# Filler matmuls in three widths, a truer count of busy PSUM banks and new priorities in a planned two-layer spectral and feed-forward kernel

## The chip, the cores and the metric

The kernel runs on one core of one Trainium2 chip. A core has five engines with queues of their own, each served in order: TensorE (PE in the profile; its weight loads are PEld), VectorE (DVE), ScalarE (ACT), GpSimd (POOL) and SyncE (SP), which issues most DMAs. Products of TensorE land in PSUM, which has 8 banks of 512 float32 columns by 128 partitions; ACT and DVE copy them from there to SBUF. The metric is the device time of one launch in microseconds, the median of several runs.

## The reference

The input x has 2048 rows (tokens) of 448 numbers. Two kinds of layer alternate, A, B, A, B, each with a residual:

```python
def _A_ref(x, w_r, w_i):              # spectral filter
    X = rfft2(x.astype(float32), axes=(-2, -1))
    X = X * (w_r + 1j * w_i)
    return irfft2(X, s=(S, D), axes=(-2, -1)).astype(bfloat16)

def _B_ref(x, w1, b1, w2, b2):        # feed-forward, 448 -> 1792 -> 448
    h = einsum("bsd,df->bsf", x, w1) + b1
    r = where(h > 0, h, 0)
    return einsum("bsf,fd->bsd", r * r, w2) + b2

x = x + _A_ref(_layernorm(x), A_w_r, A_w_i)
x = x + _B_ref(_layernorm(x), B_w1, B_b1, B_w2, B_b2)
x = x + _A_ref(_layernorm(x), A_w_r, A_w_i)
x = x + _B_ref(_layernorm(x), B_w1, B_b1, B_w2, B_b2)
```

The Fourier transform runs over all tokens, so a spectral layer needs the last token of the layer before it.

## The kernel before

The transforms are products with constant matrices, all in bf16 with float32 sums in PSUM. The 2048 tokens are 16 tiles of 128. A spectral layer goes through these steps, each a few matmuls into a PSUM tile and a copy out of it on ACT or DVE (`EV` says which engines may take it):

- A1 (first layer) or A2 (second): a first radix step over the tokens, with the layer norm's factor folded into the matrix `Fs`; result `XA`.
- TD: the transform over the 448 columns, per frequency pair p; result `U`.
- B: the second radix step; result `EF`.
- W: the product with the complex weights, on DVE alone; result `Z`. M mirrors half of the weights for it, in the first layer.
- Bi: the inverse of B; result `VT`.
- TI and AI: the inverse of the column transform (copied out to `tmp` by ACT) and of the first radix step, for one or two token tiles at a time, added to the residual x_sb on DVE at L994. ln: the layer norm's numbers, the transpose of these tokens into `yT` (matmuls with `J_sb` for the first two token tiles, DMA transposes for the others).

The feed-forward goes through h (hidden blocks of 128: four groups c of four token tiles; the first group in two halves, `h0.0.0` and `h0.0.2`, with matmuls of 256 columns; the others in pairs of half-height matmuls of 512 columns; ReLU on ACT at L631, square on DVE at L666) and o (per token tile 14 matmuls of 448 columns; the sum with the residual on DVE at L1135). In the first feed-forward, A2 of a token tile follows on its o. In the second, its rows are stored.

Nothing of the order on an engine is written out. The program is first recorded as operations (`_Op`) with their true dependencies, grouped in units (`_Unit`; a unit of PE is the chain of matmuls into one PSUM tile or a few), each with a cost in ns. `schedule` then plays the kernel through in planned time. At each step it looks, per engine, at the units whose predecessors are placed, works out when each could start (operands ready, engine free, for PE a bank free), keeps those within `look` of the earliest, and takes the one with the highest priority. A unit's priority is the longest planned path behind it, plus a bias by kind of step and layer (`PR`), plus an adjustment by its tag (`ADJ`; the tag `TI0.4` is step TI, layer 0, token tile 4; `h0.0.0` layer 0, group 0, half 0). Priority counts only among units that may start at nearly the same time. The bank of a PSUM tile is picked in the same loop (`pick_banks`), from the planned time `bank_free` at which each bank comes free. On the chip, the first matmul into a tile waits for the true readers of the tile that had the bank before.

The same loop puts in dummy matmuls: when PE's next unit starts long after PE is free, it inserts matmuls of a block of ones (`warm_mm`, L1238) into a free bank. Nothing reads them; they keep TensorE active. `used` holds the planned times in which PE was at work, dummies included. `cold_until` is 8000 ns: before that, the plan takes a dummy at twice its time.

Of the kernel before, what the change touches and what calls it, by code (L numbers as in the profile page):

```python
# [34 lines left out]
def make_constants():  # L35
# [64 lines left out]
    for g, M in enumerate((cl * np.cos(th), cl * np.sin(th))):  # L100
# [8 lines left out]


PR = {'A1': 65800.0, 'A1step': 7500.0, 'TD': [48800.0, -113100.0], 'B': [36300.0, -23900.0], 'W': [76300.0, 35800.0], 'Bi': [21700.0, 28400.0], 'step': [16400.0, 1100.0], 'M': 33500.0, 'aux': -104400.0, 'ramp': [210200.0, 192900.0], 'rstep': [2800.0, 6700.0], 'late': [85200.0, 100700.0], 'lstep': [5400.0, 6200.0], 'TI': [53500.0, 42800.0], 'AI': [44600.0, 400.0], 'h': [57700.0, -6500.0], 'A2': -27100.0, 'xb': 113100.0}
ADJ = {"": 6701, "A1.0": 29257, "A1.1": 17447, "A1.2": 16379, "A1.3": 23248, "A1.4": 19707, "A1.5": 21681,
       "A1.6": 23426, "A1.7": 1783, "A2.0": 3983, "A2.1": 24182, "A2.10": -59216, "A2.11": -3532, "A2.12": -36244,
       "A2.13": -45335, "A2.14": 47820, "A2.15": 139734, "A2.2": 1038, "A2.3": -3066, "A2.4": -12568, "A2.5": -8452,
       "A2.6": -4047, "A2.7": 1978, "A2.8": 10431, "A2.9": 63588, "AI0.0": 68353, "AI0.1": 897, "AI0.10": 516,
       "AI0.12": -5956, "AI0.14": -67415, "AI0.2": -38654, "AI0.4": -19829, "AI0.6": -15078, "AI0.8": -3605,
       "AI1.0": -20686, "AI1.1": 5286, "AI1.10": 1100, "AI1.12": -1141, "AI1.14": 13691, "AI1.2": 8647,
       "AI1.4": 59291, "AI1.6": 54430, "AI1.8": 6345, "B0.0": 19136, "B0.1": 115640, "B0.2": 22993, "B0.3": 75809,
       "B0.4": 5158, "B0.5": -4397, "B0.6": -8848, "B0.7": -51758, "B1.0": -113802, "B1.1": -60488, "B1.2": -51246,
       "B1.3": -110840, "B1.4": -102695, "B1.5": -50678, "B1.6": 21521, "B1.7": -91417, "Bi0.0": 96550,  # L120
       "Bi0.1": 144608, "Bi0.2": -84722, "Bi0.3": 90659, "Bi0.4": 115575, "Bi0.5": 64595, "Bi0.6": 43560,
       "Bi0.7": 5502, "Bi1.0": 27868, "Bi1.1": 58049, "Bi1.2": 174789, "Bi1.3": 85322, "Bi1.4": 51663,
       "Bi1.5": 84773, "Bi1.6": 122291, "Bi1.7": 95285, "M.0": -32582, "M.1": -77962, "M.2": -68639, "M.3": 11620,
       "M.4": -46400, "M.5": -52498, "M.6": -28578, "TD0.0": 62885, "TD0.1": 53127, "TD0.2": 30685, "TD0.3": 20599,
       "TD0.4": 45748, "TD0.5": 6280, "TD0.6": -18691, "TD0.7": -26835, "TD1.0": -26881, "TD1.1": -47123,
       "TD1.2": -62851, "TD1.3": -61189, "TD1.4": -81728, "TD1.5": -152870, "TD1.6": -80437, "TD1.7": -77952,
       "TI0.0": 37017, "TI0.1": -736, "TI0.10": -2254, "TI0.12": 51203, "TI0.14": 50504, "TI0.2": -15325,
       "TI0.4": 50369, "TI0.6": 10302, "TI0.8": -66186, "TI1.0": 4491, "TI1.1": 3839, "TI1.10": -18554,
       "TI1.12": -107791, "TI1.14": -62712, "TI1.2": -15113, "TI1.4": 24227, "TI1.6": -31726, "TI1.8": -63713,
       "W0.0": -3627, "W0.2": 11084, "W0.4": -35444, "W0.6": -72978, "W0.7": -86496, "W1.0": 87646, "W1.2": 77648,  # L130
       "W1.4": 114799, "W1.6": 49655, "W1.7": 28094, "aux": -45173, "h0.0.0": 19527, "h0.0.2": 78856,
       "h0.1.0": 106321, "h0.2.0": -90133, "h0.3.0": 65659, "h1.0.0": 15793, "h1.0.2": 2885, "h1.1.0": 56706,
       "h1.2.0": 30843, "h1.3.0": 25208, "ln0.0": 12199, "ln0.1": -1793, "ln0.10": 5272, "ln0.12": 6757,
       "ln0.14": -2830, "ln0.2": 61906, "ln0.4": 6787, "ln0.6": -5943, "ln0.8": -612, "ln1.0": 1193, "ln1.1": 5862,
       "ln1.10": 30854, "ln1.12": 26593, "ln1.14": -57295, "ln1.2": 10235, "ln1.4": -19457, "ln1.6": 28337,
       "ln1.8": 65496, "o0.0": -10899, "o0.1": -31999, "o0.10": -18100, "o0.11": -15446, "o0.12": -23168,
       "o0.13": -7449, "o0.14": -17614, "o0.15": -23139, "o0.2": -32228, "o0.3": -23571, "o0.4": -25779,
       "o0.5": -21180, "o0.6": -19238, "o0.7": -16528, "o0.8": -28787, "o0.9": -21480, "o1.0": 41922, "o1.1": -13364,
       "o1.10": 16273, "o1.11": 113849, "o1.12": 38097, "o1.13": 61656, "o1.14": 72389, "o1.15": 26660,
       "o1.2": 24314, "o1.3": -19452, "o1.4": 54106, "o1.5": -30131, "o1.6": 31837, "o1.7": -19040, "o1.8": 49988,  # L140
       "o1.9": 20532, "xbln0.0": -1222, "xbln0.1": -297, "xbln0.10": -57869, "xbln0.12": -15841, "xbln0.14": 4467,
       "xbln0.2": -3853, "xbln0.4": -57430, "xbln0.6": -22322, "xbln0.8": -3189, "xbln1.0": -17529,
       "xbln1.1": -10627, "xbln1.10": -2861, "xbln1.12": 67706, "xbln1.14": 22722, "xbln1.2": -8750,
       "xbln1.4": -9401, "xbln1.6": 58720, "xbln1.8": -23621}
STAY = 3000.0
LOOK = {'act': 0.0, 'dve': 50.0, 'pe': 0.0}
EV = {'A1': ['act'], 'A2': ['act'], 'TD': ['act', 'dve'], 'B': ['act', 'dve'], 'Bi': ['act', 'dve'], 'Bi0': ['act', 'dve'], 'TI': ['act'], 'M': ['act', 'dve'], 'T': ['act', 'dve'], 'XR': ['pool'], 'FS': ['pool'], 'FS2': ['dve'], 'XN': ['act', 'dve']}
SPLIT = (1, 2, 4)
NFLIP = 2
# [2 lines left out]


class _Op:
    __slots__ = ("eng", "fn", "deps", "has_dep", "ticket", "is_dma", "dsem", "cost", "lat", "unit", "gdeps", "alt", "tile")

    def __init__(self, eng, fn, is_dma, cost, lat):
        self.eng = eng
        self.fn = fn
        self.deps = []  # L160
        self.gdeps = []
        self.has_dep = False
        self.ticket = None
        self.is_dma = is_dma
        self.dsem = None
        self.cost = cost
        self.lat = lat
        self.unit = None
        self.alt = None
        self.tile = None  # L170

    def semkey(self):
        if self.is_dma:
# [61 lines left out]
class _Sched:  # L235
# [6 lines left out]
    DMA_RATE = 400.0  # L242
    TURN = 100.0
    BEGIN = 800.0

    def __init__(self):
        self.ops = {e: [] for e in self.ENGINES}
# [12 lines left out]
    def add(self, eng, fn, reads=(), writes=(), is_dma=False, cost=100.0, lat=130.0, unit=None):  # L260
# [32 lines left out]
        for a in reads:  # L293
            if isinstance(a, _PsAP):
                a.tile.readers.append(op)
        op.unit = u
        u.ops.append(op)
        return op
# [9 lines left out]
    def schedule(self):  # L308
# [88 lines left out]
        while total:  # L397
# [25 lines left out]
            if e == "pe":  # L423

                while self.warm_fn is not None:
                    gap = start - free["pe"]
                    recent = sum(min(b, free["pe"]) - max(a, free["pe"] - 3400.0) for a, b in used[-60:]
                                 if b > free["pe"] - 3400.0)
                    cold = free["pe"] < self.cold_until
                    unit = 430.0 if cold else 216.0  # L430
                    if gap < unit + (150.0 if cold or recent < self.warm_share * 3400.0 else 700.0):
                        break
                    bk = pick_banks(1, free["pe"])
                    if bk is None:
                        break
                    if bk[0] > free["pe"]:
                        free["pe"] = bk[0]
                        continue
                    d = _Op("pe", self.warm_fn(bk[1]), False, unit, 195.0)
                    old = bank_user[bk[1]]  # L440
                    if old is not None:
                        d.deps.extend(old.readers)
                    if not self.ops["pe"]:
                        d.deps.extend(self.warm_deps)
                    self.ops["pe"].append(d)
                    used.append((free["pe"], free["pe"] + unit))
                    free["pe"] += unit
                start = max(start, free["pe"] + (self.TURN if u.rows != rows else 0.0))
                rows = u.rows
# [20 lines left out]
            for op in u.ops:  # L470
# [3 lines left out]
                if op.is_dma:  # L474
                    dma_free = max(dma_free, t + 1800.0) + op.lat
                    done[op] = dma_free
                for a in (op.gdeps if e != "pe" else ()):
                    if a.tile is not None:
                        for i in range(a.tile.bank, a.tile.bank + a.tile.n):
                            bank_free[i] = max(bank_free[i], t + op.lat)  # L480
            if e == "pe":
                used.append((start, t))
            free[e] = t
            for v in order[u]:
                left[v] -= 1
                if left[v] == 0:
                    enter(v)
        self.length = max(done.values())
        self.done = done
        for e in self.ENGINES:  # L490
            for op in self.ops[e]:
# [32 lines left out]
def bass_interleave_layers__spectral_gfnet__dense_activation_squared_relu__prompt_kernel(nc, A_x, A_w_r, A_w_i, B_x, B_w1, B_b1, B_w2, B_b2, out):  # L524
# [6 lines left out]
    with ExitStack() as es:  # L531
# [702 lines left out]
        ffn(True)  # L1234


        def warm_mm(b):
            return lambda e: e.matmul(ps[:, b, :], ones[:], ones[:, None, :].to_broadcast([P, 4, P]), start=True,  # L1238
                                      stop=True)

        sch.warm_fn = warm_mm
# [75 lines left out]
```

## Time and the profile before

| what | value |
|---|---|
| median of 3 runs | 283.35 us (282.05 to 284.42) |
| profiled execution, time | 282.04 us |
| profiled execution, span | 279.5 us |
| mean granted TensorE clock | 0.994 |
| busy PE, DVE, ACT, POOL | 262.2, 213.5, 182.1, 13.2 us |
| dummy matmuls | 18 |

The span goes from the first to the last instruction of the program. The busy time of PE counts matmuls with modelled ends; they are pipelined, so a matmul of 256 columns has a duration of 0.28 us in a row while one follows another every 0.11 to 0.12 us. A chain line names the engine and line that the end waited for, followed back from the last instruction. In a row of a table by stage, the figures are the stretch, its length, the busy time and count of instructions for each engine, the granted TensorE clock as a share of full speed, the busy share of the DMA engines and GB/s. L612 is the helper that records every matmul, L637 and L638 are the copies out of PSUM on ACT and on DVE or POOL, and L666 is the helper for two-operand arithmetic.

### The profile page before, as it was taken

The numbers are of one execution on the slowest core, as the hardware profiler recorded it, in microseconds if no ns is written. First come the engines' busy times: TensorE is split into PE (matmuls) and PEld (weight loads), VectorE is DVE, ScalarE is ACT, GpSimd is POOL, SyncE is SP. The second block draws the span as 40 slices with busy tenths as digits, with TensorE's granted clock in tenths as the row PEclk, the third lists the DMA queues.
The fourth block names the chain that finished last, engine by engine and source line by source line (L and its number), as shares of the span: only waits on it lengthen the run. The fifth ranks groups of instructions, "written<-read, shape, count | busy, mean of one in ns | idle before, by whom it ended". The sixth has DMA issues, their size and how long they took to land.

```text
span 279.5 us, 5600 instructions
## 1 busy us (share of the span) xinstructions
PE 262.2 (94%) x2021; PEld 161.9 (58%) x2024; DVE 213.5 (76%) x740; ACT 182.1 (65%) x386; POOL 13.2 (5%) x28
## 2 busy tenths in 40 slices
PE   7699998799999999999997879879999999999996
PEld 2487745578655445586556545658855444554444
DVE  5958997989999977946998799399999775221542
ACT  2598986989568994376215998699836987000830
POOL 5840000000000000000000000000000000000000
PEclk9999999979999999999999999999999999999999
DMA  7999700020133030000000000002044230111001
GB/s 262 339 381 308 181 9 0 2 39 18 22 79 71 8 70 0 2 1 2 0 0 0 2 0 4 0 4 39 18 93 105 38 75 2 49 35 49 0 20 49
DMA packets 28543, 16.61 MB, mean 59 GB/s; under 512 B 21826, under 2 KB 27170, under 8 KB 28388
## 3 DMA queue, kind: packets, MB, share of 16 engines
q1 hardware_dynamic: 28084, 15.50, 20.5%
q10 hardware_dynamic: 432, 0.75, 0.7%
q8 instruction: 16, 0.26, 0.4%
q14 instruction: 11, 0.09, 0.1%
HBM read 10.75 MB, written 1.84 MB: 45 GB/s over the span
## 4 chain that ended last, share of the span: by engine, by line
PE 77%; DVE 13%; ACT 4%; DMA 2%; issue 2%; POOL 0%; ACTq 0%; DVEq 0%; POOLq 0%
PE ps L612 77%; DVE tmp L666 6%; DMA FA_sb<-c_FA 2%; DVE arena L666 2%; ACT arena L637 1%; DVE x_sb L994 1%; ACT tmp L637 1%; DVE x_sb L1135 1%; DVE W_sb L749 1%; ACT VT L1018 1%; DVE st L768 0%; DVE yT L638 0%; ACT VT L637 0%; DVE arena L638 0%; POOL Fs L649 0%
## 5 line engine op out<-in xcount | busy, mean ns | idle before, releaser
L612 PE MATMUL ps<-yT,W_sb 64*128 64x512 bf16 (+1 forms) x770 | 91.2, 349 | 0.7 <-DVE yT L638 0.4
L612 PE MATMUL ps<-W_sb,arena 128*128 128x448 bf16 (+1 forms) x476 | 86.8, 341 | 0.0
L612 PEld LDWEIGHTS ps<-yT,W_sb 64*128 64x128 bf16 (+1 forms) x770 | 54.9, 96 | 33.3 <-ACT arena L631 1.9
L631 ACT ACTIVATE arena<-ps,b1col 128x512 bf16<-128x512 f32 x84 | 52.2, 686 | 28.6 <-PE ps L612 28.5
L612 PEld LDWEIGHTS ps<-W_sb,arena 128*128 128x128 bf16 x476 | 46.0, 98 | 37.4 <-DVE arena L666 1.0
L666 DVE TENSOR_TENSOR arena<-arena 128x512 bf16<-128x512 bf16 (+1 forms) x140 | 49.7, 369 | 21.4 <-ACT arena L631 20.9
L1135 DVE SCALAR_TENSOR_TENSOR x_sb<-ps,arena 128x448 bf16<-128x448 f32 (+1 forms) x26 | 15.3, 588 | 23.4 <-PE ps L612 23.0
L637 ACT ACTIVATE arena<-ps 128x896 bf16<-128x896 f32 (+1 forms) x37 | 24.9, 746 | 2.4 <-PE ps L612 2.3
L631 ACT ACTIVATE mv<-mv,epst 128x2 f32<-128x2 f32 (+1 forms) x38 | 11.3, 299 | 22.5 <-DVE mv L769 20.9
L637 ACT ACTIVATE XA<-ps 128x512 bf16<-128x512 f32 x32 | 17.6, 594 | 9.8 <-PE ps L612 9.7
L1018 ACT ACTIVATE VT<-x_sb 128x448 bf16<-128x448 bf16 x32 | 18.3, 573 | 6.3 <-DVE x_sb L994 6.0
L637 ACT ACTIVATE VT<-ps 128x512 bf16<-128x512 f32 (+1 forms) x32 | 17.2, 590 | 4.9 <-PE ps L612 4.7
L631 ACT ACTIVATE arena<-ps 128x256 bf16<-128x256 f32 x56 | 18.5, 399 | 2.2 <-PE ps L612 1.5
L666 DVE TENSOR_TENSOR tmp<-tmp,Wt 128x896 bf16<-128x896 bf16 (+1 forms) x32 | 15.9, 560 | 0.0
L612 PE MATMUL ps<-yT,VT 64*128 64x512 bf16 x42 | 15.8, 376 | 0.0
L612 PE MATMUL ps<-arena,G_sb 128*128 128x448 bf16 (+1 forms) x72 | 14.0, 332 | 1.6 <-ACT arena L637 1.0
L637 ACT ACTIVATE tmp<-ps 128x896 bf16<-128x896 f32 (+1 forms) x18 | 14.1, 829 | 1.6 <-PE ps L612 1.6
L612 PE MATMUL ps<-HS_sb,arena 128*128 128x512 bf16 x61 | 14.8, 380 | 0.2
L612 PE MATMUL ps<-TI_sb,VT 112*128 112x112 bf16 (+1 forms) x128 | 9.8, 224 | 3.6 <-DVE VT L638 0.7
L994 DVE SCALAR_TENSOR_TENSOR x_sb<-ps,x_sb 128x448 bf16<-128x448 f32 x16 | 9.4, 619 | 3.3 <-PE ps L612 3.3
L658 ACT ACTIVATE arena<-x_sb,mv,rstd 128x448 bf16<-128x448 bf16 x10 | 7.6, 759 | 5.7 <-DMA yT<-arena 4.1
L768 DVE BATCH_NORM_STATS2 st<-xin 128x6 f32<-128x448 bf16 x16 | 9.4, 606 | 2.3 <-DMA xin<-in_A_x_dram 2.3
(84 smaller groups left out, 309.7 us busy)
## 6 DMA issues: line engine op xcount, KB each, us to landing
out_dram<-x_sb SPq DMA_DIRECT2D x15, 112.0 KB, 1.7
W_sb<-in_B_w_dram SPq DMA_DIRECT2D x1, 1568.0 KB, 15.3
W_sb<-in_B_w_dram SPq DMA_DIRECT2D x1, 1344.0 KB, 11.4
HS_sb<-c_HS SPq DMA_DIRECT2D x1, 1024.0 KB, 6.0
xin<-in_A_x_dram SPq DMA_DIRECT2D x2, 448.0 KB, 5.7
G_sb<-c_G SPq DMA_DIRECT2D x1, 672.0 KB
xin<-in_A_x_dram ACTq DMA_DIRECT2D x1, 448.0 KB, 5.8
yT<-in_A_w_r_dram SPq DMA_DIRECT2D x1, 392.0 KB
```

The lines of the kernel that those rows point to most:

```text
L612: return sch.add("pe", lambda e: e.matmul(_res(o), lhsT, rhs, start=start, stop=stop, skip_group_check=skip), [lhsT, rhs], [o], cost=cost, ...
L631: sch.add("act", lambda e: e.activation(o, _res(i), func, **kw), rd, [o], cost=c)
L637: op = sch.add(engs[0], lambda e: e.activation(o, _res(i), ACT.Copy) if h[0].eng == "act" else e.tensor_copy(o, _res(i)), [i], [o], cost=c ...
L658: op = sch.add(engs[0], lambda e: e.activation(o, i, ACT.Identity, bias=b, scale=s) if h[0].eng == "act" else e.tensor_scalar(o, i, s, b, ...
L666: sch.add(eng, lambda e: e.tensor_tensor(o, _res(a), b, op), [a, b], [o], cost=_free(o) / rate + 69.0)
L749: small(lambda e, c=c, lo=lo: e.scalar_tensor_tensor(out=lo, in0=_res(c), scalar=-1.0 / D, in1=lo, op0=ALU.mult, op1=ALU.subtract), [c, lo ...
L768: small(lambda e, si=si, xi=xi: e.bn_stats(si, xi), [xi], [si], _free(xi) / 0.96 + 69.0)
L994: small(lambda e, xx=xx, xi=xi, r=r, i=i: e.scalar_tensor_tensor(out=xx, in0=_res(r), scalar=1.0, in1=xi, op0=ALU.mult, op1=ALU.add, accum ...
L1018: sch.add("act", lambda e, i=i, o=o, x=x: e.activation(o, x, ACT.Square, accum_out=sd[:, i, 1:2]), [x], [o, sd[:, i, 1:2]], cost=560.0)
L1135: small(lambda e: e.scalar_tensor_tensor(out=o, in0=_res(i), scalar=r[0] if r else 1.0, in1=xb[:, t, d0:d1], op0=ALU.mult, op1=ALU.add), [ ...
```

## The change

Four things change; the operations and their dependencies stay.

- Dummy matmuls come in 512, 256 or 128 columns. The plan looks at the use of PE in the 3413 ns (`WINDOW`) before the next unit's start, the gap itself counted as empty. Where that is under 70% (`warm_share`, unchanged), or in the cold start, it fills every gap of at least 120 ns with the widest dummy that leaves 60 ns. Where it is 70% or more, it puts in none.
- A bank is busy until the operations that read its tile end (`takes`). Before, each operation of another engine held up the banks of all matmuls among its dependencies, those with which it shares only an SBUF buffer included, and for a bank that meanwhile belonged to another tile too.
- All adjustments of `ADJ` are new, and some ten times larger.
- `LOOK` for PE goes from 0 to 50 ns.

```diff
-ADJ = {"": 6701, "A1.0": 29257, ...
+ADJ = {"": -580138, "A1.0": 899030, ...
-       "AI1.0": -20686, ... "TI0.2": -15325, "TI0.4": 50369, ... "TI1.4": 24227, ...
+       "AI1.0": -14810, ... "TI0.2": -21187, "TI0.4": -62986, ... "TI1.4": -1225233, ...
-       "h0.0.0": 19527, "h0.0.2": 78856, ... "ln1.0": 1193, ... "ln1.2": 10235, ...
+       "h0.0.0": 783048, "h0.0.2": 600819, ... "ln1.0": 976430, ... "ln1.2": 2049490, ...
 STAY = 3000.0
-LOOK = {'act': 0.0, 'dve': 50.0, 'pe': 0.0}
+LOOK = {'act': 0.0, 'dve': 50.0, 'pe': 50.0}
...
+    WINDOW = 3413.0
...
         for a in reads:
             if isinstance(a, _PsAP):
                 a.tile.readers.append(op)
+                op.takes.append(a.tile)
...
                 while self.warm_fn is not None:
                     gap = start - free["pe"]
-                    recent = sum(min(b, free["pe"]) - max(a, free["pe"] - 3400.0) for a, b in used[-60:]
-                                 if b > free["pe"] - 3400.0)
                     cold = free["pe"] < self.cold_until
-                    unit = 430.0 if cold else 216.0
-                    if gap < unit + (150.0 if cold or recent < self.warm_share * 3400.0 else 700.0):
+                    recent = sum(min(b, start) - max(a, start - self.WINDOW) for a, b in used[-90:]
+                                 if b > start - self.WINDOW)
+                    if gap < 120.0 or not (cold or recent < self.warm_share * self.WINDOW):
                         break
-                    bk = pick_banks(1, free["pe"])
+                    n = next((n for n in (512, 256, 128) if (n / 2.4 + 2.5) * (2.0 if cold else 1.0) + 60.0 <= gap), 0)
+                    bk = pick_banks(1, free["pe"]) if n else None
                     if bk is None:
                         break
                     if bk[0] > free["pe"]:
                         free["pe"] = bk[0]
                         continue
-                    d = _Op("pe", self.warm_fn(bk[1]), False, unit, 195.0)
+                    unit = (n / 2.4 + 2.5) * (2.0 if cold else 1.0)
+                    d = _Op("pe", self.warm_fn(bk[1], n), False, unit, 195.0)
...
-                for a in (op.gdeps if e != "pe" else ()):
-                    if a.tile is not None:
-                        for i in range(a.tile.bank, a.tile.bank + a.tile.n):
-                            bank_free[i] = max(bank_free[i], t + op.lat)
+                for w in op.takes:
+                    for i in range(w.bank, w.bank + w.n):
+                        bank_free[i] = max(bank_free[i], t + op.lat)
...
-        def warm_mm(b):
-            return lambda e: e.matmul(ps[:, b, :], ones[:], ones[:, None, :].to_broadcast([P, 4, P]), start=True,
+        def warm_mm(b, n):
+            return lambda e: e.matmul(ps[:, b, 0:n], ones[:], ones[:, None, :].to_broadcast([P, n // P, P]), start=True,
                                       stop=True)
```

The longest remaining path enters every priority, and `PR` and the constants in the program (22,000 per group for h, 5,500 per token tile for o) are as before.

## What I predict, and why

> **What bounds the kernel now.** I read the page first (busy shares, the row of the granted clock, the chain that ended last), then cut the span into stages and asked for the busy time of each.
>
> ```profile
> PE 262.2 (94%) x2021; PEld 161.9 (58%) x2024; DVE 213.5 (76%) x740; ACT 182.1 (65%) x386; POOL 13.2 (5%) x28
> PEclk9999999979999999999999999999999999999999
> PE 77%; DVE 13%; ACT 4%; DMA 2%; issue 2%; POOL 0%; ACTq 0%; DVEq 0%; POOLq 0%
> ```
>
> TensorE is busy for 94% of the span and holds 77% of the chain. One slice of the clock row is below 9. The chain leaves TensorE for DVE and ACT in short pieces only. The table by stage shows where (columns: stretch, length, busy time and instructions of PE, PEld, DVE, ACT and POOL, granted clock, DMA share, GB/s).
>
> ```profile
> 0.00:8.80 8.80, 5.37 (x16) 1.94 (x16) 5.34 (x19) 2.08 (x4) 4.77 (x12) 1.00 0.80 296
> 8.80:47.00 38.20, 36.56 (x273) 25.95 (x275) 33.44 (x91) 33.39 (x64) 8.46 (x17) 1.00 0.69 203
> 47.00:56.60 9.60, 7.07 (x87) 5.86 (x88) 7.33 (x37) 8.65 (x20) 0.00 (x0) 1.00 0.01 2
> 56.60:60.10 3.50, 3.50 (x20) 2.52 (x18) 3.08 (x11) 2.75 (x7) 0.00 (x0) 0.51 0.39 75
> 60.10:147.80 87.70, 87.34 (x666) 53.20 (x664) 75.54 (x300) 55.24 (x125) 0.00 (x0) 1.00 0.11 22
> 147.80:154.20 6.40, 4.37 (x53) 3.91 (x51) 5.09 (x24) 3.80 (x8) 0.00 (x0) 1.00 0.00 0
> 154.20:179.20 25.00, 21.91 (x165) 12.51 (x167) 21.52 (x49) 21.14 (x35) 0.00 (x0) 1.00 0.01 2
> 179.20:187.80 8.60, 6.74 (x84) 5.58 (x84) 6.48 (x30) 7.76 (x18) 0.00 (x0) 1.00 0.00 1
> 187.80:277.10 89.30, 89.30 (x668) 50.39 (x668) 55.28 (x182) 47.26 (x108) 0.00 (x0) 1.00 0.18 44
> ```
>
> The two feed-forward stages (60.1 to 147.8 and 187.8 to 277.1) are solid: 87.34 of 87.70 and 89.30 of 89.30. No order of work takes time out of them while their matmuls stay the same. Idle PE lies in five places: 38.20 - 36.56 = 1.64 in the first spectral layer, 2.53 in its ramp into the feed-forward (47.0 to 56.6), 2.03 at the layer boundary, 3.09 in the second spectral layer, 1.86 in its ramp: 11.15 us in all, beside 8.8 us before the first real matmul and 2.4 us behind the last. In the stretch 56.6 to 60.1 PE is never idle, but the clock is 0.51.
>
> **The clock dip.** The windows around it, and the matmuls in it:
>
> ```profile
> 49.80:53.20 3.40, 2.75 (x38) 1.00 0.02 5
> 53.20:56.60 3.40, 1.55 (x20) 1.00 0.00 0
> 152.20:155.60 3.40, 1.80 (x30) 1.00 0.02 5
> L612 PE MATMUL ps<-yT,W_sb 128*128 128x256 bf16 x16 | 3.5, 408 | 0.0
> L612 PE MATMUL ps<-yT,W_sb 128*128 128x256 bf16 x224 | 26.6, 282 | 0.4 <-DVE yT L638 0.4
> ```
>
> PE was busy for 1.55 of the 3.40 us just before the dip. [...] The price two ways: 3.50 x (1 - 0.51) = 1.7 us of lost clock; and 16 matmuls of 256 columns cover 3.5 us where the average over all 224 is 26.6 / 224 = 0.119 us, so 1.9 us: 1.6 lost. What follows is solid to 147.8, so the whole 1.7 us stands on the path.
>
> **The change, part by part.**
>
> *Dummies by recent use.* Before, one width (512 columns), only in a planned gap of at least 366 ns after low use, or 916 ns after high use. After: any planned gap of at least 120 ns, in the widest of 512, 256 and 128 that leaves 60 ns, as long as the planned use of the last 3413 ns, the gap counted as empty, is under 70%; above that none. The kernel before issues 18:
>
> ```profile
> L1238 PE MATMUL ps<-ones 128*128 128x512 bf16 x18 | 6.0, 496 | 1.9 <-POOL ones L679 1.9
> 1.88 5.37 PE L1238 MATMUL ps<-ones 128*128 128x512 bf16 x16 [1.88 <-POOL ones L679]
> 153.07 0.40 PE L612 MATMUL ps<-Fs,tmp 128*128 128x128 bf16 x4 [1.05 <-DVE tmp L675]
> L612 PE MATMUL ps<-Fs,tmp 128*128 128x128 bf16 x64 | 5.4, 219 | 1.3 <-DVE tmp L675 1.0 <-DVE x_sb L1135 0.2
> ```
>
> 16 stand at the start, two later, and none in the ramp before the dip. At the start nothing changes much: they fill time before the first data. A 128-column matmul costs (0.40 - 0.22) / 3 = 0.06 us of PE, its weight load beside it. The troughs hold 11.15 us of idle time, so at most some 180 dummies of the narrowest width. Cover: they lie in time in which PE waits for DVE and ACT, so I take 0 for them. Without that cover (the operand comes earlier on the chip than planned) the next real matmul waits for the rest of one dummy, 0 to 0.06 us of a narrow one. Each dummy also waits for the readers of the tile that its bank held, and everything on PE is queued behind it; as the plan takes that bank as free, I take 0 here too. Upper bound for both: 96 fills (11.15 / 0.116, a narrow dummy and its 60 ns) of 0.06 us, 5.8 us. What they bring: the ramp before the dip goes from 1.55 of 3.40 busy towards 70%, above the 1.80 that brought no dip; the boundary is filled by the same rule. I take the whole 1.7 us.
>
> *The bank count.* Before, each ACT, DVE or POOL instruction marked as busy the banks of every matmul it depends on, also of those whose SBUF operand it only overwrites, long after that bank had gone to another tile. After, it marks the banks it reads. No instruction or wait on the chip goes with this; the real waits were by true readers already. It only makes the plan truer, in the stretches where banks decide. The waits of PE in the ramp and in the second spectral layer:
>
> ```profile
> PE ps L612 <- ACT tmp L637: 1.4, 3, 0.5
> PE ps L612 <- DVE VT L638: 0.7, 1, 0.7
> PE ps L612 <- ACT arena L637: 1.7, 4, 0.7
> PE ps L612 <- ACT VT L637: 1.1, 2, 0.7
> ```
>
> The 1.4 us on ACT's copies out of PSUM in the first ramp are largely inverse transforms that read only VT, ready long before: a wait for a bank, and open to a better order. The 1.7 us in the second layer mixes banks with data.
>
> *The priorities.* The adjustments went from about 0.17 million at most to 2.0 million, against some tens of thousands between the constants of PR, and a remaining path that can't exceed the plan's length (some 280,000). So the adjustment alone now decides between units that can start together. One reading: h0.0.0 had 57,700 + 88,000 + 19,527 = 165,227, level with TI0.4 (85,200 - 21,600 + 53,500 + 50,369 = 167,469) and below TI0.2 (242,775). Now it has 928,748 against 54,114 and 236,913. In the second ramp ln1.0 and ln1.2 gain 0.98 and 2.05 million while TI1.4 loses 1.23 million. So the steps of the first tokens go ahead of the inverse transforms of later ones on ACT, DVE and PE. The chain in both ramps:
>
> ```profile
> 49.18 1.18 DVE x_sb L994 x4
> 56.39 60.24 PE ps L612 x460
> 181.24 0.02 issue
> 181.26 1.18 DVE x_sb L994 x4
> 187.80 89.34 PE ps L612 x668
> ```
>
> From the first residual to the solid stretch it takes 7.2 us in the first ramp and 6.5 in the second, with PE's 2.53 and 1.86 us of idle time inside. The boundary is a real barrier: nothing of the second spectral layer can start ahead of the last token's chain, so I leave its 2.03 us. In the second spectral layer DVE is the bound (21.52 of 25.00 with its wait for the first products), and its arithmetic stays; 1 of the 3.09 us may go. Bounds for order and banks together: all idle time but the boundary's, 9.1 us, at the one end; at the other a loss of 2 us, about what the troughs would grow by if each of the two ramps slipped by half its present idle time. I take 2.0, a little under half of the two ramps' 2.53 + 1.86, because these are the rows with bank waits and with the clearest change of order.
>
> *The rest.* PE's look-ahead of 50 ns only lets it pick a unit that starts up to 50 ns later: in the solid stretches there is nothing to lose, so 0. SP's queue: the loads at the start share one tag, so their order among themselves is kept; transposes, the two bias rows and stores may move among each other. DMA share is 0.01 in the second spectral layer and 0.11 to 0.18 in the feed-forward stages, so 0; were a transpose late, the solid stretches would show it. In POOL's queue the scaled factors now outrank the copies of xr, and both are needed by the same matmuls: 0, within the 1.64 us of the first layer.
>
> **The sum**, against the profiled execution: 279.5 - 1.7 - 2.0 = 275.8 us of span. The profiled execution took 282.04, 2.5 us around its span, so 278.3. That execution is the fastest of those shown; the median is 283.35, and the difference of 3.7 taken from it gives **279.6**, or 1.3% less. About 1% is what a measurement of this kernel can tell from no change.
>
> [...]
>
> **Rivals.**
> 1. *The clock is mended, the order brings nothing.* For it: DVE and ACT are near their limits in the troughs (ACT 8.65 of 9.60 and 7.76 of 8.60), so another order may only move the waits. Against: the bank waits. Time: 283.35 - 1.7 = 281.7.
> [...]
> 3. *Slower: fillers ahead of real work.* PE takes its queue in order, so in the troughs a dummy, or a later token's unit put first by the new order, that still waits for its bank or for ACT holds up a ready matmul of the critical ramp. Place: 47 to 57 and 154 to 188. Price: the bound above, 5.8 us for fillers, with the 1.7 us of clock still gained: 283.35 + 4.1 = 287.5. It decides as soon as the holdups exceed 3.7 us. For: 11.15 us of troughs are exactly where the plan's errors gather. Against: the two late dummies of before stand in such a place and cost nothing visible; a narrow one is 0.06 us.
>
> Chances: the forecast (both gains, with more or less of the order's) 0.53; rival 1 0.15; rival 2 0.15; rival 3 0.17. Faster by over 1% (under 280.5): 0.53 of the forecast's cases and a little of the rest, less its own lower end, so 0.54. Within 1%: 0.30, most of rivals 1 and 2. Slower by over 1%: 0.16. The low end takes 5.8 of the order's bound of 9.1 us with the clock: 283.35 - 7.5 = 275.8. The high end reaches into the slower rival, 286.0. The forecast's own range is 276 to 281.
>
> **What would show it.** The clock row without a 7 in the second eighth of the span, and 1.00 right after the first ramp; 40 to 150 matmuls on ones, most of them narrow, in the troughs; the solid stretches as long as before, within 0.5 us; the first ramp's solid stretch at about 54.5 to 55.5 instead of 56.4; less wait on ACT tmp. Wrong would be: the half clock somewhere else, the solid stretches with idle time (a late transpose, a bank), or ramps that last longer than 7.2 and 6.5 us.

## The result, and the profile after

The changed kernel takes 274.94 us (median of 4 runs, 274.71 to 275.0) against 283.28 of the kernel before (282.05 to 284.42): a ratio of 0.9705, 95% interval 0.9664 to 0.9746. The forecast was 279.6 with a low end of 275.8: the right side, a change too small by more than half, and a result below the low end. The profiled execution took 274.93 us, its span is 272.9.

The page of the changed kernel: busy shares, the clock row, the chain, and the dummies' group.

```profile
PE 261.2 (96%) x2038; PEld 158.9 (58%) x2038; DVE 212.2 (78%) x742; ACT 182.1 (67%) x384; POOL 13.2 (5%) x28
PEclk9999999999999999999999999999999999999999
PE 78%; DVE 16%; DMA 3%; issue 1%; ACT 1%; POOL 0%
L1244 PE MATMUL ps<-ones 128*128 128x512 bf16 (+1 forms) x32 | 9.7, 440 | 1.9 <-POOL ones L685 1.9
```

The 7 in the clock row is gone. There are 32 dummies, 16 of them in the cold start as before, and all but one are 512 wide. The table by stage, cut at the same events as that of before (columns as there):

```profile
0.00:8.90 8.90, 5.31 (x16) 1.91 (x16) 5.33 (x21) 2.38 (x5) 4.75 (x12) 1.00 0.80 297
8.90:46.00 37.10, 36.39 (x275) 26.14 (x275) 32.20 (x90) 33.07 (x62) 8.47 (x17) 1.00 0.71 207
46.00:53.00 7.00, 5.75 (x76) 5.03 (x76) 5.60 (x26) 6.43 (x14) 0.00 (x0) 1.00 0.01 2
53.00:142.80 89.80, 89.48 (x691) 52.66 (x692) 79.85 (x326) 59.99 (x138) 0.00 (x0) 1.00 0.13 24
142.80:149.00 6.20, 5.61 (x59) 4.33 (x56) 5.05 (x24) 3.62 (x8) 0.00 (x0) 1.00 0.01 3
149.00:174.10 25.10, 22.66 (x174) 12.93 (x173) 22.00 (x50) 20.28 (x34) 0.00 (x0) 1.00 0.00 1
174.10:180.80 6.70, 6.31 (x77) 5.10 (x78) 4.62 (x21) 6.03 (x13) 0.00 (x0) 1.00 0.01 4
180.80:270.50 89.70, 89.67 (x680) 50.81 (x677) 57.15 (x190) 50.29 (x113) 0.00 (x0) 1.00 0.20 43
```

The two ramps are what shrank: the first from 9.60 us to 7.00, the second from 8.60 to 6.70. The first spectral layer is 1.1 shorter, the dip's 3.50 us of half clock are gone. The boundary, the second spectral layer (25.00 and 25.10) and the second solid stretch are as long as before to within 0.4 us; so is the first one, once the dip's loss is taken off its 3.50 + 87.70. The chain of the changed kernel, the same events as those shown of before and one more:

```profile
48.81 1.18 DVE x_sb L1000 x4
...
61.61 4.41 DMA yT<-x_sb
66.02 0.05 issue
66.07 76.70 PE ps L618 x588
...
176.14 0.64 DVE x_sb L1000 x2
...
180.38 90.10 PE ps L618 x685
```

From the first residual to the hidden matmuls it is now 4.2 us instead of 7.7 in the first ramp (48.81 to 53.0) and 4.7 instead of 6.5 in the second (176.14 to 180.82). New in the chain is a DMA transpose that lands at 66.0, which the feed-forward waits for. It is the one for token tiles 2 and 3, and the new order issues it later, at 61.61; in the kernel before it stood at 55.38:

```profile
55.38 1.34 SPq L599 DMA_TRANSPOSE yT<-x_sb  x1
```

### The profile page after: what moved, and what is told of

It is laid out like the page before. It is cut to its first block, busy times and chain, and to the rows that moved or that the text cites. A ratio compares the mean times of both kernels' runs of the same rounds, so it can differ in the third digit from the quotient of the medians.

```text
span 272.9 us, 5620 instructions
## 1 busy us (share of the span) xinstructions
PE 261.2 (96%) x2038; PEld 158.9 (58%) x2038; DVE 212.2 (78%) x742; ACT 182.1 (67%) x384; POOL 13.2 (5%) x28
## 4 chain that ended last, share of the span: by engine, by line
PE 78%; DVE 16%; DMA 3%; issue 1%; ACT 1%; POOL 0%
PE ps L618 78%; DVE tmp L672 5%; DVE arena L672 2%; DVE x_sb L1000 2%; DVE st L774 2%; DMA yT<-x_sb 2%; DMA xin<-in_A_x_dram 1%; DVE yT L644 1%; DVE arena L644 1%; DVE x_sb L1141 1%; DVE VT L672 0%; ACT VT L643 0%; POOL Fs L655 0%; PE ps L1244 0%; DVE mv L775 0%
## 5 line engine op out<-in xcount | busy, mean ns | idle before, releaser
L618 PE MATMUL ps<-yT,W_sb 64*128 64x512 bf16 (+1 forms) x770 | 89.3, 346 | 0.7 <-DVE yT L644 0.3
L618 PEld LDWEIGHTS ps<-yT,W_sb 64*128 64x128 bf16 (+1 forms) x770 | 51.5, 95 | 36.6 <-DMA yT<-x_sb 0.8
L664 ACT ACTIVATE arena<-x_sb,mv,rstd 128x448 bf16<-128x448 bf16 x11 | 8.4, 764 | 7.3 <-DMA yT<-arena 5.5
L1244 PE MATMUL ps<-ones 128*128 128x512 bf16 (+1 forms) x32 | 9.7, 440 | 1.9 <-POOL ones L685 1.9
```

The lines of the kernel that those rows point to most:

```text
L618: return sch.add("pe", lambda e: e.matmul(_res(o), lhsT, rhs, start=start, stop=stop, skip_group_check=skip), [lhsT, rhs], [o], cost=cost, ...
L664: op = sch.add(engs[0], lambda e: e.activation(o, i, ACT.Identity, bias=b, scale=s) if h[0].eng == "act" else e.tensor_scalar(o, i, s, b, ...
L1244: return lambda e: e.matmul(ps[:, b, 0:n], ones[:], ones[:, None, :].to_broadcast([P, n // P, P]), start=True, stop=True)
```

## The experiments

Their line numbers are their own. "Old" is the kernel before, "new" the changed one. Three theories were open: that the order of the work is most of the gain (O), that the dummies and the clock are (D), or that the truer bank count is, whatever the priorities (B).

### The clock: e1, e2, e3, e11

**e1**, the kernel before, unedited. 

> The kernel before once more, for the granted clock and the span of each execution. Theory O (the order of the work is most of the gain; the clock dip is a term of its own of 1.5 to 1.7 us that comes once or twice per execution, by where idle stretches fall): spans of 279 to 282 us, the shorter ones with a mean clock of 0.994 (one dip), the longer ones with 0.988 (two). Rival D (the dip comes from the dummies' absence and is in every execution alike): one clock, 0.994, in all, and the spread of 282 to 284 us comes from elsewhere.

Measured: 283.91 us against 284.33 (ratio 1.0002, 0.9977 to 1.0028). Every execution has dips, and the time goes by their number. In 63 executions of this kernel (e1 and the ones beside three sets of experiments), 9 had a mean clock of 0.994 and spans of 279.5 to 279.9 us, 22 had 0.987 or 0.988 and 280.1 to 281.4, and 32 had 0.982 and 281.7 to 282.7: one, two and three dips, each some 1.1 to 1.5 us. (A dip of 3.5 us at a clock of 0.51 takes 0.006 off the mean of such a span, so the mean counts them; kept traces show one and two, three is read from the mean.) The profiled execution of e1 has two, and not where the first profile had its one (windows of PE: length, busy time, clock, DMA share, GB/s):

```profile
149.80:153.20 3.40, 1.55 (x24) 1.00 0.00 0
153.20:156.70 3.50, 3.50 (x24) 0.51 0.02 5
183.90:187.30 3.40, 1.95 (x26) 1.00 0.02 5
187.30:190.80 3.50, 3.32 (x16) 0.51 0.39 75
```

They follow the idle stretches at the layer boundary and in the second ramp, with none in the first ramp (clock 1.00 in every stage up to 147.8 us). This fits theory O, whose dips come by where idle stretches fall, and not rival D's one dip alike in all executions.

**e3**, old order and banks with the new dummy rule alone.

```diff
-                    if gap < unit + (150.0 if cold or recent < self.warm_share * 3400.0 else 700.0):
+                    if gap < 120.0 or not (cold or recent < self.warm_share * self.WINDOW):
```

> The kernel before with the new rule for dummies alone (25 of them instead of 18, two in the first ramp just ahead of the dip, none at the layer boundary); order and banks as before. Theory O: at most the dip of the first ramp goes, 281.6 to 283.3 us. Rival D: most of the 8 us comes with the dummies, below 279 us.

Measured: 282.44 us, ratio 0.994 (0.9908 to 0.9972). Three of ten executions have no dip and spans of 278.1 to 278.3, two have one (279.2 and 279.4), five have two (280.6 to 281.1); none has three, where 17 of the 33 executions of the old kernel in the same set have. The two dummies at 53.21 in its timeline stand in the first ramp's idle stretch, and raise its busy time from 1.55 to 1.96 of 3.40 us:

```profile
53.21 0.60 PE L1240 MATMUL ps<-ones 128*128 128x512 bf16 x2
53.71 0.57 PE L614 MATMUL ps<-TI_sb,VT 112*128 112x112 bf16 x8
54.70 0.57 PE L614 MATMUL ps<-TI_sb,VT 112*128 112x112 bf16 x8 [0.42 <-ACT tmp L639]
55.78 0.22 PE L614 MATMUL ps<-J_sb,x_sb 128*128 128x128 bf16 x1 [0.51 <-ACT tmp L639]
56.50 0.56 PE L614 MATMUL ps<-tmp,FI_sb 128*128 128x224 bf16 x4 [0.50 <-ACT tmp L639]
56.89 0.87 PE L614 MATMUL ps<-yT,W_sb 128*128 128x256 bf16 x6
```

So the dummies alone are worth about one dip of three. That it is the first ramp's is read from where they stand, and isn't shown: 1.96 us is hardly more than the 1.95 us busy in the stretch that the second dip of e1 followed. And 278.1 is the span of the old order without a dip, against which orders can be compared: the new one's is 272.9, 5.2 us less.

**e2**, the new kernel with its 16 late dummies left out of PE's queue, the order otherwise the same.

```diff
-                    self.ops["pe"].append(d)
+                    if cold:
+                        self.ops["pe"].append(d)
```

> The changed kernel with the 16 dummies behind the cold start left out of PE's queue; order, banks and all else are the same. Theory O: the first ramp has no dummy in it anyway, so its clock stays 1.00; the layer boundary (146 to 149 us) gets as idle as in the kernel before, so a dip follows there in some of the executions and costs up to 1.7 us: 275 to 276.6 us. Rival D (dummies are what mends the clock, and worth several us): a dip in every execution, 276.6 us or more.

Measured: 275.94 us (274.94 to 277.01), ratio to before 0.9712 (0.968 to 0.9745). Three of six executions have a clock of 0.994 and spans of 274.4 to 275.1, three have 1.00 and 273.0 to 273.5. As O said: the gain stays, and a dip comes back in half of the executions. The kept trace is of an execution without a dip, so its place isn't recorded. The stretch that probably invites it is the idlest of that trace, at the layer boundary, without and with the dummies (e2, then the new kernel):

```profile
146.00:149.40 3.40, 1.28 (x19) 1.00 0.00 0
```

```profile
146.00:149.40 3.40, 2.81 (x29) 1.00 0.00 0
```

**e11**, the new kernel with the old dummy rule, which puts 8 late dummies, three of them at the boundary. 

> The changed kernel with the old rule for dummies (8 behind the start instead of 16, none in the second ramp, one in the first; all 512 wide; order the same). Theory O with windows (only the stretch at the layer boundary is idle enough for a dip, and three dummies there, or seven, both cover the fullest part of it): spans of 272.9 to 273.1 us and a clock of 1.00 in all or nearly all executions, 275 us. Rival W (the stretch needs all of the new rule's dummies): a dip in a third or more of the executions, spans up to 275.1, as without late dummies.

Measured: 275.16 us (274.98 to 275.44), ratio to before 0.9684 (0.9647 to 0.9721); spans of 272.9 to 273.4 and a clock of 1.00 in all six. With the new order the old rule does nearly as well: the three widths and the new condition are worth about 0.2 us here, by medians taken on different chips.

### The parts of the plan: e4, e5, e6

**e4**, the old kernel with the new bank count alone.

```diff
-                for a in (op.gdeps if e != "pe" else ()):
-                    if a.tile is not None:
+                for w in op.takes:
```

> The kernel before with the new count of busy banks alone, priorities and dummy rule as before. Theory O with the addition that priorities were fitted to the count they were made with: no gain alone, slower by 3 to 6 us (286 to 289 us), the loss in the troughs. Rival B (the truer count is what brings the gain, whatever the priorities): faster by 3 us or more, under 280 us.

Measured: 289.13 us, 1.0177 of before (1.0128 to 1.0226). Theory B falls. The loss is not in the troughs, where I had looked for it: in its chain it is in the first feed-forward, which waits for a transpose and, up to 90.55, for DVE's work behind it:

```profile
72.00 11.75 PE ps L613 x69
83.75 4.67 DMA yT<-arena
...
90.55 63.86 PE ps L613 x484
```

**e5**, the new kernel with the old `ADJ`. 

> The changed kernel with the priorities of the kernel before; dummy rule, bank count and look-ahead stay new. Theory F (priorities and bank count were fitted to each other, and only the pair is fast): 282 to 286 us, and the first ramp ends (first matmul on yT and W_sb) at about 56 us, not at 53. Rival B (the truer count and the look-ahead carry the gain): under 278 us.

Measured: 282.11 us, 0.9939 (0.9869 to 1.001); span 279.6 without a dip, first hidden matmul at 55.89.

**e6**, the new kernel with the old bank count. 

> The changed kernel with the old count of busy banks; priorities, dummy rule and look-ahead stay new. Theory F: slower than the kernel before, 286 to 292 us, the loss not in the first ramp (its solid stretch at 54 to 55 us) but in the second half. Rival P (the priorities alone carry the gain): under 278 us.

Measured: 288.82 us, 1.0176 (1.0101 to 1.025). The first ramp ends at 53.71, nearly as early as in the new kernel, and the time is lost in both feed-forwards: 100.6 us instead of 96.0 from there to the second layer, 94.9 instead of 89.7 from the first hidden matmul of the second (188.81) to the last matmul. I had looked for it in the second half alone. Neither piece of the plan is worth much without the other: e5 is the only one of the three that isn't slower than before, and its ratio can't be told from 1. But e4 and e5 share the old priorities and the new count, and lie 7 us apart; only one dip of this is clock. They differ in the dummy rule, which also moves the plan, and in PE's look-ahead. No run has the look-ahead alone, so what it is worth stays open.

### Where the order gains: e7, e8, e12

These join two plans. Each layer half begins with work that needs all of what is ahead of it, so the queues of the engines can be cut there, and one part taken from the new plan with its banks, the rest from the old:

```diff
+        self.ops = {e: [op for k, mode in enumerate(PARTS) for op in plans[mode][0][e] if op.part == k]
+                    for e in self.ENGINES}
```

**e7**, new first ramp and feed-forward. 

> The order and the banks of the kernel before everywhere except in the first ramp and feed-forward, up to and with A2, which are taken over from the changed kernel; the new dummy rule throughout. Against e3, which is this with the old order there too: theory O (the first ramp is the largest piece) has the stretch from the first inverse transform to the first hidden matmul shorter by 2.5 to 3 us, 0.5 us of it given back by a wait for a DMA transpose, and a span of 275.4 to 276.2 us in executions without a dip, against 278.1. Rival E (the gain is spread and belongs to the first spectral layer and the later stages, which a ramp only passes on): less than 1 us.

Measured: 278.6 us, 0.9827 (0.9775 to 0.988); spans without a dip 275.8, 276.1 and 276.4, so 1.7 to 2.3 under e3 (one lies above the range expected). From the first inverse transform to the first hidden matmul it takes 7.0 us instead of 9.8 (47.12 to 54.16, against 47.11 to 56.89), and 0.8 of it, not 0.5, is given back in the feed-forward.

**e8**, new second ramp and feed-forward. 

> The same, with the second ramp and feed-forward taken over from the changed kernel instead. Theory O: the second ramp is shorter by 1.6 to 2.0 us, the feed-forward as long as before or 0.3 us longer, so a span of 276.2 to 276.7 us without a dip. Rival E: less than 1 us.

Measured: 280.02 us, 0.9862 (0.9811 to 0.9913); without a dip 276.4 and 277.3. From residual to hidden matmul 4.68 us (181.57 to 186.25) instead of 6.53 in e3: 1.85 less. The second of the two spans lies 0.9 above the first and above the range expected; these runs don't show why.

**e12**, new first spectral layer. 

> The order and banks of the kernel before, with the first spectral layer (everything ahead of the first ramp) taken over from the changed kernel; the new dummy rule throughout. From the times of the first residual in the traces (49.29 us in e3, 48.81 in the changed kernel) the layer itself is worth 0.5 us: a span of 277.4 to 277.8 us without a dip. Rival E (the first layer also hands over a better state to the ramp, and carries what e7 and e8 left over): 276.6 us or less. Besides: the time outside the span was 2.5 us in kernels with the old first layer and 2.0 in those with the new one; if it goes with the first layer, it is 2.0 to 2.1 here.

Measured: 281.5 us, 0.99 (0.9846 to 0.9953), with dips in all four executions. The first residual comes at 48.05 us (e3: 49.29), and everything up to the second layer is 1.24 earlier. More than the 0.5 that I had read off: the new ramp starts its first residual later by the rest, which hid it. With one dip the span is 278.4, against 279.2 and 279.4 in e3. The time outside the span is 1.8 us (e3: 2.4 to 2.6), so it does go with the first layer; why, these runs don't show.

### Why the ramp is shorter: e9, e10

**e9**, e5 with `ADJ["h0.0.0"] = 783048`. 

> The kernel of e5 (new dummies, bank count and look-ahead, old priorities) with one adjustment, that of h0.0.0, raised to its new 783,048. Reading H (the prediction's: the first hidden unit had been outranked by later inverse transforms): the first hidden matmul comes earlier than e5's 55.89 us, by 1 us or more. Reading N (it was outranked by nobody, it waits for the layer norm of token tile 1): within 0.2 us of e5's, and the same time, 282.1 us.

**e10**, e5 with the nine new `ln0` adjustments. 

> The kernel of e5 with the 9 new adjustments of ln0 alone. Reading N (the layer norms of token tiles 0 and 1 waited on ACT behind squares of tiles 2 and 3 and copies of later transforms): the square root of tile 1 comes some 2 us earlier and the first hidden matmul at about 54.3 us instead of 55.89; the time stays at 281.5 to 283 us, as tiles 2 and later come later and the feed-forward waits for them. Reading H: the first hidden matmul stays at 55.7 to 56.

Measured: 282.12 us for e9 (0.996, 0.9919 to 1.0002), its first hidden matmul at 55.88, against e5's 55.89: nothing. For e10 282.57 us (0.9955, 0.9925 to 0.9985), its first hidden matmul at 54.27. Its feed-forward gives it back: 99.5 us from there to the second layer (54.27 to 153.73) instead of e5's 97.5. What held the ramp is largely in ACT's queue. The kernel before (VT from x_sb is the sum of squares of a token tile, mv from mv with one element its square root, tmp from ps a copy for an inverse transform):

```profile
49.85 0.58 ACT L1018 ACTIVATE VT<-x_sb 128x448 bf16<-128x448 bf16 x1
50.33 0.19 ACT L1018 ACTIVATION_READ_ACCUMULATOR VT<-x_sb 128x1 f32 x1
50.42 0.90 ACT L637 ACTIVATE tmp<-ps 128x896 bf16<-128x896 f32 x1
51.22 0.28 ACT L631 ACTIVATE mv<-mv 128x1 f32<-128x1 f32 x1
51.40 0.48 ACT L637 ACTIVATE yT<-ps 128x384 bf16<-128x384 f32 x1
51.77 0.57 ACT L1018 ACTIVATE VT<-x_sb 128x448 bf16<-128x448 bf16 x1
...
52.33 0.57 ACT L1018 ACTIVATE VT<-x_sb 128x448 bf16<-128x448 bf16 x1
...
52.89 0.56 ACT L1018 ACTIVATE VT<-x_sb 128x448 bf16<-128x448 bf16 x1
...
53.45 0.28 ACT L631 ACTIVATE mv<-mv 128x1 f32<-128x1 f32 x1
```

The new kernel:

```profile
49.82 0.61 ACT L1024 ACTIVATE VT<-x_sb 128x448 bf16<-128x448 bf16 x1
50.29 0.23 ACT L1024 ACTIVATION_READ_ACCUMULATOR VT<-x_sb 128x1 f32 x1
50.38 0.60 ACT L1024 ACTIVATE VT<-x_sb 128x448 bf16<-128x448 bf16 x1
50.85 0.23 ACT L1024 ACTIVATION_READ_ACCUMULATOR VT<-x_sb 128x1 f32 x1
50.94 0.50 ACT L637 ACTIVATE mv<-mv 128x1 f32<-128x1 f32 x2
51.32 2.54 ACT L643 ACTIVATE tmp<-ps 128x896 bf16<-128x896 f32 x3
```

The square root of the second token tile came at 53.45, behind copies and squares for later tiles; now it stands at about 51.1, straight behind the two squares, and the copies follow. The hidden matmuls need both tiles. Reading N holds for the start of the hidden matmuls, and with it the limit of a single early step: e10 moves the roots up to 52.25 and gains nothing in the end.

## Why the prediction failed, step by step

- **The bound and the places**: right. The solid stretches kept their length, the boundary and the second spectral layer too (24.1 us from the first TD to TI in e3, 24.2 in the new kernel); the gain is in the ramps and the first layer.
- **The term "order and banks", 2.0 us, is the one that was mis-sized**: it measured 5.3 (span 278.15 to 272.87). Its pieces: first spectral layer 1.2, where I took nothing; first ramp 2.7 and second ramp 1.85, where I took 2.0 for both; 0.4 given back in the feed-forwards. What in the order shortens the first layer and the second ramp was not traced further. I had taken "a little under half" of the ramps' idle time, 2.53 and 1.86. That pot was too small, for two reasons: the busy time of short bursts holds modelled ends, and matmuls can leave the ramp. One group in the first ramp, of the kernel before (47.0 to 56.6) and of the new one (46.0 to 53.0):

```profile
L612 PE MATMUL ps<-TI_sb,VT 112*128 112x112 bf16 x48 | 3.2, 213 | 1.5 <-DVE mv L675 0.6 <-DVE yT L638 0.6 <-ACT tmp L637 0.3
L618 PE MATMUL ps<-TI_sb,VT 112*128 112x112 bf16 x40 | 2.6, 212 | 0.0
```

  48 matmuls are busy for 3.2 us, 0.067 each; in an unbroken burst, 16 of them (at 186.12 in the kernel before) take 0.96 us from first start to last end, so (0.96 - 0.21) / 15 = 0.05 each. Over this group alone 0.8 us of "busy" is by this estimate the ends of broken bursts, and belongs to the pot. And the new ramp has 8 of these matmuls less: they run at 59.89, inside the feed-forward, some 0.4 us of PE's work that is moved and not saved. The share, too, was a guess between 0 and all. The chain's 7.2 us would have been the better guide, for 2.5 us of them are copies of inverse transforms in ACT's queue:

```profile
53.64 0.90 ACT tmp L637
...
54.72 1.62 ACT tmp L637 x2
```

- **The clock, 1.7 us**: the size of a dip was a little high (measured 1.1 to 1.5). That a stretch fuller than 1.80 us is safe, as I took it, was wrong: a dip followed 1.95 (e1). Nor does the busy time of 3.4 us alone tell where one comes: in the kernel before, none followed the 1.57 us at the layer boundary (150.6 to 154.0) in the first profile, and one the 1.55 us there in e1. Which measure of use decides stays open. The number of dips was wrong: I took one from the median. The median execution before has two, and many have three: some 2.7 and 4 us. Subtracting from the median what was counted in the luckiest execution is the error.
- **Who mended it**: partly wrong. In the first ramp, where I let the dummies do it, the new kernel has none; the order leaves no idle stretch there (5.75 busy of 7.00). At the boundary it is probably the dummies: without the late ones a dip came back in half of e2's executions, though no trace shows it there.
- **How many dummies**: 40 to 150 narrow ones forecast, 16 late ones, one of them 256 wide, the others 512. There is little to fill.
- **The bank waits**: the 1.4 us on ACT's copies, which I read as waits for a bank, are gone from the new ramp; no run tells a wait for a bank from ACT's queue there. Of the numbers beside them, ln1.2 gains 2.04 million and TI1.4 loses 1.25, not 2.05 and 1.23.
- **PE's look-ahead, 0**: open, as no run has it alone (e4 and e5).
- **h0.0.0 ahead of TI0.2**: wrong (e9). What counts there is the layer norms of the first tokens on ACT (e10); by tag I had named layer norms for the second ramp alone, and the first tokens' steps on ACT only in general.
- **Outside the span**: taken as 2.5 us, measured 2.0.
- **SP's queue, 0**: 0.3 us too good, PE's idle time just before 66.07 (0.7 in e7). The transpose that lands at 66.0 is the late one that I named as a sign of error. The ramp that ended earlier is only part of it: the new order, which puts token tiles 0 and 1 first, issues the transpose of tiles 2 and 3 6.2 us later than before.
- **Rivals**: the slower one, fillers ahead of real work, didn't show: with and without the late dummies the undisturbed span is 272.9 and 273.0. That an order brings nothing, or that the dip stays, is out.

The account: two dips in the median, 280.8 - 278.1 = 2.7; order 5.3; outside the span 0.5. Together 8.5, measured 8.3. The low end had room for 5.8 of the order, so the order alone did not break the range; the second dip and the time outside the span did. That the median of these four executions has two dips, by its time, and not three is chance: beside the later sets the kernel before took 283.9 to 284.5 us.

## What to carry to other kernels

Where a median and a profile of the same kernel differ, find out first which of several executions was profiled: list span and clock of each, and count a clock loss as often as the median execution has it. In a ramp, follow one token's chain through the queue of the engine that is nearly full, here ACT, and see which entries ahead of it belong to later tokens: that, and not the idle time of the engine that waits, says what an order can gain. Priorities and the model that they were fitted with are one thing; the new bank count in the old kernel (e4), or the new priorities with the old count (e6), was 14 us slower than the changed kernel, and the new count, look-ahead and dummies with the old priorities (e5) 7 us.

## What I had not expected of the hardware

- In the first profile the half clock (0.51 over 3.5 us) came after a stretch of 3.4 us in which TensorE worked in short bursts for a bit under half of the time (1.55 busy), with no gap above 0.56 us; with two dummies of 512 columns in that stretch (1.96 busy in e3's trace) none of ten executions had a third dip. In e1 dips followed 1.55 us at the layer boundary and 1.95 us in the second ramp.
- Its place moves between executions of the same program (56.6 us in the first profile, 153.2 and 187.3 in e1), and so does the number of dips, so that one kernel has spans of 279.5 to 282.7 us, in steps of 1.1 to 1.5.
